# Half of the turned tiles by VectorE in batches 1 to 3, and an order planned with other durations and random shakes

## The chip, the core and the metric

The program runs on one core of a Trainium2 chip. The metric is the device time of one execution in microseconds (us). The core has five engines that work side by side, each through its own list of instructions in order: TensorE (PE) multiplies matrices, VectorE (DVE) and ScalarE (ACT) work on tiles elementwise and along rows, GpSimd (POOL) does elementwise work too, and SyncE (SP) issues the DMA transfers here. An instruction starts when those ahead of it on its engine have been issued and the semaphores it waits for are up.

## The reference

Attention over 4 batches, 8 heads, 576 positions and 64 columns, with a threshold in the softmax, and two feed-forward blocks behind it, all in float32:

```
scores = scale * q @ k.T                     # each batch and head: 576 x 576
thresh = max(scores, -1) - tau
scores = where(scores >= thresh, scores, -1e9)
attn   = softmax(scores);  x = attn @ v      # x: 2304 tokens x 512
h = x @ w_in;  x = (h * clip(h + 3, 0, 6) / 6) @ w_out      # 512 -> 2048 -> 512
h = x @ w_in2; x = (h * sigmoid(1.702 * h)) @ w_out2
```

## The kernel before

**Tiles and stages.** Two heads are one unit, a head pair; there are 4 batches of 4 head pairs. A head pair has nine score tiles of 128 queries by 576 keys: four of its first panel (queries 0 to 255 of both heads), four of its second panel (256 to 511), and a rest tile with the last 64 queries of both. For each tile PE makes the scores (`ps`), DVE takes the row maximum (`nm`, L621) and a threshold from it (`th`), ACT the exponential (`e`, L626), DVE masks it and sums (L627), POOL divides (L640). The tile must then be turned, keys onto partitions, into the buffer `et`, and PE multiplies it with v (`av`, L737, in batch 0; `av_`, L756, in the other batches). The feed-forward blocks work on the transposed result: the first half of block 1 (`moe_a`) runs beside the attention of the next batch, its second half (`moe_b`) and block 2 (`moe2`) behind attention. There each product of two float32 numbers is three matmuls of their high and low parts.

**Turning.** PE turns 128 x 128 pieces with the identity as the other operand (`trans`, L678) into a PSUM bank, and ACT copies the bank to `et` (L681). The other way is `blocks`: DVE turns 32 x 32 blocks of four tiles into the tile `tr` (L699), SP writes `tr` to a scratch tensor in DRAM (`turned`, L702) and reads it back in four transfers, so that the blocks come to lie in their place in `et` (L704); only the last 64 keys go over PE (`last_keys`). `TURNED = (2, 3)` names the batches in which both panels of every head pair go this second way; batch 1 takes `plain`, where PE turns all, and batch 0 has a function of its own, `turn`. In the batches of `TURNED` the threshold is made by ACT (L623), else by DVE (L625). From batch 1 on there is one `et` buffer, `ets[1]`, for all head pairs, five buffers for `e` and three for the raw q and k tiles (`qk`, loaded at L545 and L546).

**What sets the order.** Nothing is executed where it is written. `add` and `move` enter each operation into a plan with its engine, a cost in ns, a nominal time and the buffers that it reads and writes; a `move` enters SP's issue (590 ns) and a transfer whose cost is its bytes divided by 360. `Plan.order` plays the plan through, each engine taking the ready operation with the lowest key; `Plan.latest` plays it backwards and gives new keys. `settle` does both three times, and then, for each seed in `KICKS`, shakes the keys within a random stretch of the plan with `kicked` and does both again. `KICKS` is empty here. `fill` puts dummy products of the tile `two` (L1135) into every gap of PE in the plan that is wide enough. The order so found is fixed when the program is built.

Of the kernel before, what the change touches and what calls it, by code (L numbers as in the profile page):

```python
# [32 lines left out]

KICKS = ()

# [226 lines left out]
def tile_top_attention_moe_moe2(  # L262
# [87 lines left out]
    def pe(n):  # L350
        return 7 + 0.43 * n

# [132 lines left out]
    QC = S + 64  # L485
    TURNED = (2, 3)
    turns = [(dram.tile([P, 2048], F32, name="turned"), mark()) for _ in range(2)]
# [8 lines left out]

    def et_m(p):
        return ets[1].t[:, 2560 * p:2560 * p + 2048].rearrange("p (a h k t j) -> p a h k t j", a=4, h=2, k=4, t=2)

    def et_p(p):  # L500
        return ets[1].t[:, 2560 * p:2560 * p + 2048].rearrange("p (h k n) -> p h k n", h=2, k=4)

    def et_4(p):
        return ets[1].t[:, 2560 * p + 2048:2560 * p + 2560].rearrange("p (h n) -> p h n", h=2)

    def et_r():
        return ets[1].t[:, 5120:].rearrange("p (h k n) -> p h k n", h=2, k=5)

# [3 lines left out]
    def unit(u, b, j, t0):  # L512
# [4 lines left out]
        def K(name, s=0):  # L517
            return t0 + 2700 * s + NOMINAL[name]
# [63 lines left out]
        def score1(s):  # L582

            ps, (hd, m) = buf("ps", 2, "ps", [P, 2, 512]), tiles[s]
            q0 = 256 * hd + m * P

            def mm():
                for i in range(2):
                    nc.tensor.matmul(ps.t[:, i, :SH], f32(qzb.t)[:, q0:q0 + P], f32(khb.t)[:, i * SH:(i + 1) * SH], start=True, stop=True)

            add(PE, 4 * 243, K("S", s), "S", mm, [(qzb, x) for x in (("z", hd), (hd, 0))] + [khb], [ps])
            soft(s, ps)

        def score(ss):

            if len(ss) == 1 and tiles[ss[0]] is not None:
                return score1(ss[0])
            pss = {s: buf("ps", 2, "ps", [P, 2, 512]) for s in ss}

            def mm():  # L600
                for i in range(2):
                    for s in ss:
                        t = tiles[s]
# [3 lines left out]
            add(PE, 4 * 243 + 300 + 40 * (len(ss) > 1), K("S", ss[0]), "S", mm, [qhb, khb], [pss[s] for s in ss])  # L607
            for s in ss:
                soft(s, pss[s])

        def soft(s, ps):
# [9 lines left out]
            add(DVE, 665, K("R", s), "R", lambda: nc.vector.tensor_reduce(out=nm.t[:, c], in_=ps.t[:, :, :SH], op=ALU.max, axis=AX.XY, negate=True), [ps], [(nm, s)])  # L621
            if b in TURNED:
                add(ACT, 150, K("TH", s), "TH", lambda: nc.scalar.activation(out=th.t[:, c], in_=nm.t[:, c], func=ACTF.Identity, scale=-1.0, bias=nt_b.t), [(nm, s), nt_b], [(th, s)])  # L623
            else:
                add(DVE, 121, K("TH", s), "TH", lambda: nc.vector.tensor_scalar(out=th.t[:, c], in0=nm.t[:, c], scalar1=-1.0, scalar2=nt_b.t, op0=ALU.mult, op1=ALU.add), [(nm, s), nt_b], [(th, s)])  # L625
            add(ACT, 624, K("X", s), "X", lambda: nc.scalar.activation(out=ev(), in_=ps.t[:, :, :SH], func=ACTF.Exp, bias=nm.t[:, c]), [ps, (nm, s)], [e])  # L626
# [55 lines left out]

        def last_keys(p, ss):
            trans([(s, 4, tiles[s][0] * 256 + tiles[s][1] % 2 * P) for s in ss], 512, lambda kn: (et_4(p)[:kn], lambda x: x.rearrange("p (h n) -> p h n", h=2)), ets[1], (p, 4), ss[-1])

        def plain(p, ss):
            for hd in range(2):
                mine = [s for s in ss if tiles[s][0] == hd]
                for k0 in (0, 2):
                    trans([(s, k0 + i, i * 256 + m * P) for i in range(2) for m, s in enumerate(mine)], 512,  # L690
                          lambda kn, hd=hd, k0=k0: (et_p(p)[:kn, hd, k0:k0 + 2], lambda x: x.rearrange("p (k n) -> p k n", k=2)), ets[1], (p, hd, k0), ss[-1])
            last_keys(p, ss)

        def blocks(p, ss):

            et, at, src = ets[1], ss[-1], buf("tr", 1, "tr", [P, 4, 2, 4, 2, 32])
            for s in ss:
                hd, t = tiles[s]
                add(DVE, dve(512), K("DT", s), "DT", lambda hd=hd, t=t % 2, e=e_of[s]: nc.vector.transpose(out=src.t[:, :, hd, :, t, :].rearrange("p g k j -> p k g j"), in_=e.t[:, :512].rearrange("p (k g j) -> p k g j", k=4, g=4)),  # L699
                    [e_of[s]], [(src, s)])  # L700
            turned, there = turns[p]
            move(K("DM", at), "DM", 16 * P * 512, lambda: nc.sync.dma_start(out=turned, in_=src.t.rearrange("p g h k t j -> p (g h k t j)")), [src], [there])  # L702
            for g in range(4):
                move(K("DM", at) + 3000, "DM", 4 * P * 512, lambda g=g: nc.sync.dma_start(out=ets[1].t[32 * g:32 * g + 32, 2560 * p:2560 * p + 2048].rearrange("p (a n) -> p a n", a=4),  # L704
                     in_=turned[:, 512 * g:512 * g + 512].rearrange("(a p) n -> p a n", a=4)), [there], [(et, ("m", p, g))])
            last_keys(p, ss)

        def turn_r():

            et, at = ets[1], 4  # L710
            trans([(4, k, k * P) for k in range(4)], 512,
                  lambda kn: (et_r()[:kn, :, 0:4].rearrange("p h k n -> p k h n"), lambda x: x.rearrange("p (k h n) -> p k h n", k=4, h=2)), et, "r", at)
            trans([(4, 4, 0)], P, lambda kn: (et_r()[:kn, :, 4], lambda x: x.rearrange("p (h n) -> p h n", h=2)), et, "r4", at)

        def turn(p, ss, rest):

            et, at = ets[0], ss[-1]
            for hd in range(2):
# [10 lines left out]
        def av(p, at):  # L729
# [8 lines left out]

            op = add(PE, 350 + 10 * (1 + 0.84 * n), K("AV", at), "AV", mm, [vs] + [(et, r) for r in regions], [pv], [xr])
            add(ACT, act(n), K("XR", at), "XR", copy(lambda: xr.t, lambda: pv.t[:, :n]), [pv], [xr])  # L740
            return op

        def av_(at):

            et, pv = ets[1], [bank(1), bank(1)]
            for x in pv:
                add(PE, 0, K("AV", at), "AV", lambda: None, [vs, et], [x], xrs.values())

            def mm():
                def x(p, k, hd):  # L750
                    return et_r()[:, hd, k] if p == 2 else et_4(p)[:, hd] if k == 4 else et_p(p)[:, hd, k] if b not in TURNED else et_m(p)[:, :, hd, k].rearrange("p a t j -> p t a j")

                for p, o, c, n in ((0, pv[0], 0, 256), (1, pv[0], 256, 256), (2, pv[1], 0, 64)):
                    for k in range(5):
                        for hd in range(2):
                            nc.tensor.matmul(o.t[64 * hd:64 * hd + 64, c:c + n], v_(k, hd), x(p, k, hd), start=k == 0, stop=k == 4)  # L756

            add(PE, 450 + 10 * (2 + 0.84 * S), K("AV", at), "AV", mm, [vs, et], pv, xrs.values())
            add(ACT, act(256), K("XR", at), "XR", copy(lambda: xrs[0].t, lambda: pv[0].t[:, :256]), [pv[0]], [xrs[0]])
            add(ACT, act(256), K("XR", at), "XR", copy(lambda: xrs[1].t[:, :256], lambda: pv[0].t[:, 256:]), [pv[0]], [(xrs[1], 0)])  # L760
            add(ACT, act(64), K("XR", at), "XR", copy(lambda: xrs[1].t[:, 256:], lambda: pv[1].t[:, :64]), [pv[1]], [(xrs[1], 1)])

# [10 lines left out]
        def full():  # L773
            for p in range(2):
                if p:
                    score2(4)
                for pair in PAIRS[p]:
                    for s in pair:
                        score2(s)
                    norm(([4] if pair[0] == 5 else []) + list(pair))  # L780
                    if pair[0] == 5:
                        turn_r()
# [281 lines left out]
    for b in range(B):  # L1064
# [9 lines left out]
        if u == FULL:  # L1074
# [6 lines left out]
            changed[-1][0].deps |= {o for o in pl.ops if any(x.pool == "stg" for x in o.bufs)}  # L1081
            for ap, r in ((lambda: et_4(0)[64:], (0, 4)), (lambda: et_4(1)[64:], (1, 4)), (lambda: et_r()[64:, :, 4], "r4")):
                add(POOL, 124 + 1.04 * 512, t, "ez", lambda ap=ap: nc.gpsimd.memset(ap(), 0.0), [], [(ets[1], r)])
        else:
# [109 lines left out]
```

## Time and profile before

| | |
|---|---|
| median of 3 runs | 1097.37 us (1097.24 to 1100.8) |
| the profiled execution | 1093.03 us, its span 1091.2 us |
| PE busy | 1058.7 us, 97% of the span |
| DVE / ACT / POOL busy | 724.2 / 638.1 / 515.3 us |
| attention ends | at about 440.7 us |

A profile is one execution. Its rows give busy times of engines, idle times with what ended them (`<-`), the chain of work that ended last, and for a DMA the time from its issue to its landing. Matmuls overlap in the array, so the duration of one (0.27 us for 128 columns) is longer than the distance from one to the next, and busy time counts overlapping ones once. A float32 product that isn't marked fp32r in the program has two records for one instruction; transposes have one. The clock column is the granted TensorE clock as a share of full speed.

### The profile page before, as it was taken

The page shows a single profiled execution, that of the slowest core. Times are in us where ns is not written, and L with a number is a line of the kernel's source. Part 1 is how long each engine was busy: PE and PEld are TensorE (multiplying, and loading weights), DVE is VectorE, ACT ScalarE, POOL GpSimd, SP SyncE. Part 2 cuts the span into 40 slices and gives each one's busy share as a digit, 9 for nine tenths or more (in the row PEclk, how much of TensorE's full clock was granted, in tenths as well). Part 3 has the DMA queues.
Part 4 walks back from the last instruction along what each step waited for, and adds up shares of the span by engine and source line. Part 5 has one row for each costly group of instructions (what it writes and reads, how often), then busy time and mean ns, then how long its engine had stood idle before and what let it go on. Part 6 is the DMA issues. An engine that isn't in the chain of part 4 may idle for free.

```text
span 1091.2 us, 20840 instructions
## 1 busy us (share of the span) xinstructions
PE 1058.7 (97%) x7706; PEld 970.0 (89%) x7706; DVE 724.2 (66%) x1485; ACT 638.1 (58%) x1340; POOL 515.3 (47%) x598
## 2 busy tenths in 40 slices
PE   8999899989898999999999999999999999999998
PEld 7677788888787989999999999989998989889888
DVE  6998766676686784467877333778787675563634
ACT  4888777765576664576555324666566665444433
POOL 3679868675686764555466224541323332001000
PEclk9999999999999999999999999999999999999999
DMA  7334222266878687445654212435545543312202
GB/s 206 116 120 129 96 68 78 91 190 176 250 213 271 200 242 195 140 137 166 203 174 145 79 48 61 132 105 183 175 137 173 167 139 102 116 46 71 92 1 73
DMA packets 90053, 150.19 MB, mean 138 GB/s; under 512 B 8928, under 2 KB 51552, under 8 KB 87904
## 3 DMA queue, kind: packets, MB, share of 16 engines
q1 hardware_dynamic: 89952, 148.87, 44.8%
q8 instruction: 60, 0.98, 0.4%
q14 instruction: 41, 0.34, 0.1%
HBM read 101.52 MB, written 47.32 MB: 136 GB/s over the span
## 4 chain that ended last, share of the span: by engine, by line
PE 69%; DVE 9%; DMA 7%; ACT 5%; POOL 4%; issue 3%; SPq 2%; POOLq 0%; DVEq 0%; ACTq 0%
PE py L835 23%; PE pm L815 14%; PE pm L972 14%; PE pm L835 6%; PE pm L756 4%; PE ps L573 4%; PE pm L678 2%; DMA qk<-in_k_dram 2%; DVE e L627 2%; DMA qk<-in_q_dram 1%; ACT e L626 1%; DVE nm L621 1%; DMA wrawstg<-in_w1i_dram 1%; POOL e L640 1%; POOL kqv L369 1%
## 5 line engine op out<-in xcount | busy, mean ns | idle before, releaser
L835 PE MATMUL py<-g,outhring 128*128 128x512 f32 (+2 forms) x1152 | 287.7, 337 | 2.6 <-DVE g L369 1.3
L835 PEld LDWEIGHTS py<-g,outhring 128*128 128x128 f32 x1152 | 193.7, 188 | 20.6 <-DVE g L369 3.3
L835 PE MATMUL py<-g,outlring 128*128 128x512 f32 (+2 forms) x576 | 193.5, 336 | 0.0
L815 PE MATMUL pm<-xh,inhring 128*128 128x256 f32 (+1 forms) x512 | 154.8, 302 | 2.3 <-DVE t L827 2.2
L815 PE MATMUL pm<-xl,inhring 128*128 128x256 f32 (+1 forms) x512 | 151.8, 296 | 0.0
L815 PE MATMUL pm<-xh,inlring 128*128 128x256 f32 (+1 forms) x512 | 151.7, 296 | 0.0
L972 PE MATMUL pm<-outhring,inhring 128*128 128x256 f32 x512 | 144.5, 282 | 1.5 <-ACT u L366 0.8
L972 PE MATMUL pm<-outlring,inhring 128*128 128x256 f32 x512 | 143.6, 281 | 0.0
L972 PE MATMUL pm<-outhring,inlring 128*128 128x256 f32 x512 | 143.5, 280 | 0.0
L621 DVE TENSOR_REDUCE nm<-ps 128x1 f32<-128x576 f32 x144 | 106.2, 750 | 34.4 <-PE ps L573 30.3
L369 POOL TENSOR_TENSOR g<-t,g 128x256 fp32r<-128x256 f32 (+1 forms) x104 | 88.1, 851 | 82.7 <-ACT g L366 79.9
L627 DVE SCALAR_TENSOR_TENSOR e<-ps,th,e 128x576 f32<-128x576 f32 x128 | 102.6, 810 | 33.2 <-ACT e L626 31.9
L827 DVE SCALAR_TENSOR_TENSOR t<-t,pm 128x256 f32<-128x256 f32 (+1 forms) x128 | 57.1, 448 | 94.0 <-ACT t L826 93.7
L835 PEld LDWEIGHTS py<-g,outlring 128*128 128x128 f32 x576 | 108.2, 188 | 10.0
L369 POOL TENSOR_TENSOR wmstg<-wmstg,wrstg 128x512 uint32<-128x512 uint32 x48 | 64.6, 1347 | 94.8 <-DVE wmstg L422 77.3
L835 PE MATMUL pm<-g,outhring 128*128 128x256 f32 (+1 forms) x512 | 107.7, 301 | 0.5 <-POOL g L369 0.4
L369 POOL TENSOR_TENSOR g<-tc,g 128x512 fp32r<-128x512 f32 x24 | 31.8, 1326 | 161.6 <-ACT g L366 154.9
L826 ACT ACTIVATE t<-pm,half 128x256 f32<-128x256 f32 (+1 forms) x128 | 63.7, 498 | 74.3 <-PE pm L815 68.6
L626 ACT ACTIVATE e<-ps,nm 128x576 f32<-128x576 f32 x128 | 93.0, 733 | 15.2 <-DVE nm L621 13.4
L815 PEld LDWEIGHTS pm<-xh,inhring 128*128 128x128 f32 x512 | 98.0, 191 | 4.2 <-DVE t L827 2.9
L972 PEld LDWEIGHTS pm<-outhring,inhring 128*128 128x128 f32 x512 | 96.8, 189 | 4.9 <-ACT u L366 1.1
L972 PEld LDWEIGHTS pm<-outlring,inhring 128*128 128x128 f32 x512 | 96.9, 189 | 2.6
(114 smaller groups left out, 2433.8 us busy)
## 6 DMA issues: line engine op xcount, KB each, us to landing
turned<-tr SPq DMA_DIRECT2D x16, 1024.0 KB, 4.5
et<-turned SPq DMA_DIRECT2D x64, 256.0 KB, 5.6
wrawstg<-in_w1i_dram SPq DMA_DIRECT2D x16, 512.0 KB, 4.0
wrawstg<-in_w1o_dram SPq DMA_DIRECT2D x16, 512.0 KB, 3.8
wrawstg<-in_w2i_dram SPq DMA_DIRECT2D x16, 512.0 KB, 3.9
wrawstg<-in_w2o_dram SPq DMA_DIRECT2D x16, 512.0 KB, 3.9
qk<-in_k_dram SPq DMA_DIRECT2D x24, 288.0 KB, 3.9
qk<-in_q_dram SPq DMA_DIRECT2D x24, 288.0 KB, 3.7
```

What stands on the lines that cost most here:

```text
L369: return lambda: (nc.vector if eng == DVE else nc.gpsimd).tensor_tensor(out=o(), in0=a(), in1=b(), op=op)
L573: nc.tensor.matmul(ps.t[:, i, :SH], qss[hd].t[:, q0:q0 + P], w[hd].t[:, i * SH:(i + 1) * SH], start=a, stop=z)
L621: add(DVE, 665, K("R", s), "R", lambda: nc.vector.tensor_reduce(out=nm.t[:, c], in_=ps.t[:, :, :SH], op=ALU.max, axis=AX.XY, negate=True), ...
L626: add(ACT, 624, K("X", s), "X", lambda: nc.scalar.activation(out=ev(), in_=ps.t[:, :, :SH], func=ACTF.Exp, bias=nm.t[:, c]), [ps, (nm, s)] ...
L627: add(DVE, 729, K("M", s), "M", lambda: nc.vector.scalar_tensor_tensor(out=ev(), in0=ps.t[:, :, :SH], scalar=th.t[:, c], in1=ev(), op0=ALU ...
L678: nc.tensor.transpose(pt.t[:kn, o:o + P], e_of[s].t[:, keys(k)], id_b.t)
L756: nc.tensor.matmul(o.t[64 * hd:64 * hd + 64, c:c + n], v_(k, hd), x(p, k, hd), start=k == 0, stop=k == 4)
L815: nc.tensor.matmul(ph.t[:, :n], a, v, start=(cc == 0 and i == 0), stop=(cc == KC - 1 and i == 2))
L826: add(ACT, 93 + act(n), K("RL"), "RL", lambda: nc.scalar.activation(out=tt_(), in_=pt(), func=ACTF.Relu, scale=1.0 / 6.0, bias=half_b.t), ...
L827: add(DVE, dve(n), K("GT"), "GT", lambda: nc.vector.scalar_tensor_tensor(out=tt_(), in0=tt_(), scalar=1.0, in1=pt(), op0=ALU.min, op1=ALU. ...
L835: nc.tensor.matmul(py.t[:, :n], a, v, start=(st and i == 0), stop=(sp and i == 2))
L972: nc.tensor.matmul(o.t[:, :n], u.t[:, ws], v.t[:, xv], start=(st and kk == 0 and i == 0), stop=(sp and kk == 1 and i == 2), skip_group_che ...
```

## The change

Three things change together. In batches 1 to 3 the first panel of each head pair goes by `blocks` (DVE and DRAM), and the second panel and the rest tile by `turn` (PE and ACT), where batch 1 had both panels on PE and batches 2 and 3 both on DVE. With it, `av_` multiplies two groups of 256 and 320 queries instead of three of 256, 256 and 64, and all thresholds are made by DVE. Second, costs of the plan are other numbers. Third, `KICKS` holds nine seeds.

```
-KICKS = ()
+KICKS = (9, 22, 44, 100, 235, 395, 771, 940, 4389)
...
 def pe(n):
-        return 7 + 0.43 * n
+        return 9 + 0.428 * n
...
-    TURNED = (2, 3)
...
-            if b in TURNED:
-                add(ACT, 150, K("TH", s), "TH", lambda: nc.scalar.activation(out=th.t[:, c], in_=nm.t[:, c], func=ACTF.Identity, scale=-1.0, bias=nt_b.t), [(nm, s), nt_b], [(th, s)])
-            else:
-                add(DVE, 121, K("TH", s), "TH", lambda: nc.vector.tensor_scalar(...
+            add(DVE, 121, K("TH", s), "TH", lambda: nc.vector.tensor_scalar(...
...
             for g in range(4):
-                move(K("DM", at) + 3000, "DM", 4 * P * 512, ...
+                move(K("DM", at) + 3000, "DM", 7 * P * 512, ...
...
-            op = add(PE, 350 + 10 * (1 + 0.84 * n), K("AV", at), "AV", mm, ...
+            op = add(PE, 150 + 10 * (1 + 0.84 * n), K("AV", at), "AV", mm, ...
...
-                for p, o, c, n in ((0, pv[0], 0, 256), (1, pv[0], 256, 256), (2, pv[1], 0, 64)):
+                for p in range(2):
                     for k in range(5):
                         for hd in range(2):
-                            nc.tensor.matmul(o.t[64 * hd:64 * hd + 64, c:c + n], v_(k, hd), x(p, k, hd), start=k == 0, stop=k == 4)
+                            x = et_a(et, 1, hd, k) if p else et_4()[:, hd] if k == 4 else et_0()[:, :, hd, k].rearrange("p a t j -> p t a j")
+                            nc.tensor.matmul(pv[p].t[64 * hd:64 * hd + 64, :CH[p][1]], v_(k, hd), x, start=k == 0, stop=k == 4)
...
-                (blocks if b in TURNED else plain)(p, ss)
+                if p:
+                    turn(p, ss, 4)
+                else:
+                    blocks(ss)
```

SP's queue in batch 2, before: `turned<-tr` is the write of a panel that DVE has turned, `et<-turned` one of the four reads of it, `qk` and `kqv` the loads of q, k and v of head pairs to come.

```order
L702 DMA turned<-tr 128x2048
L704 DMA et<-turned 32x4x512 x4
L545 DMA qk<-in_k_dram 128x576
L702 DMA turned<-tr 128x2048
L853 DMA ypd<-ys 128x256 x2
L702 DMA turned<-tr 128x2048
L704 DMA et<-turned 32x4x512 x4
L546 DMA qk<-in_q_dram 128x576
L704 DMA et<-turned 32x4x512 x4
L545 DMA qk<-in_k_dram 128x576
```

The same queue in batch 2 of the changed kernel, where line numbers are smaller by 7 to 30:

```order
L681 DMA turned<-tr 128x2048
L539 DMA qk<-in_q_dram 128x576
L736 DMA x1d<-xr_3283 128x256
L823 DMA ypd<-ys 128x256
L683 DMA et<-turned 32x4x512 x4
L552 DMA kqv<-in_vp_dram 128x640
L538 DMA qk<-in_k_dram 128x576
L823 DMA ypd<-ys 128x256
L539 DMA qk<-in_q_dram 128x576
L538 DMA qk<-in_k_dram 128x576
L823 DMA ypd<-ys 128x256
L681 DMA turned<-tr 128x2048
```

One round trip per head pair stands there where two stood, and whole groups of q and k loads lie between two round trips.

PE at the end of batch 3, before: the last product with v (`pm<-et,kqv`), the last products of `moe_a` around it (`pm<-g,out...`), and the dummies (`pm<-two`) ahead of the next stage.

```order
L835 MATMUL pm<-g,outhring_1416 128x320 x2
L835 MATMUL pm<-g,outlring_1440 128x320
L756 MATMUL pm<-et,kqv 64x256 x20
L756 MATMUL pm<-et,kqv 64x64 x10
L835 MATMUL pm<-g,outhring_1530 128x320 x2
L835 MATMUL pm<-g,outlring_1541 128x320
L835 MATMUL pm<-g,outhring_1598 128x320 x2
L835 MATMUL pm<-g,outlring_1611 128x320
L1135 MATMUL pm<-two 128x128 x4
```

The same end in the changed kernel, from the transposes of the last second panel (`pm<-id,e`):

```order
L668 MATMUL pm<-id,e 128x128 x16
L805 MATMUL pm<-g,outhring_1145 128x320 x2
L805 MATMUL pm<-g,outlring_1168 128x320
L668 MATMUL pm<-id,e 64x128 x4
L805 MATMUL pm<-g,outhring_1231 128x320 x2
L805 MATMUL pm<-g,outlring_1244 128x320
L805 MATMUL pm<-g,outhring_1328 128x320 x2
L805 MATMUL pm<-g,outlring_1342 128x320
L726 MATMUL pm<-et,kqv 64x256 x10
L726 MATMUL pm<-et,kqv 64x320 x10
```

Sixteen transposes that DVE did before now stand on PE in each head pair of batches 2 and 3, and the product with v has two shapes of ten instructions instead of thirty instructions; two dummies (`L1105 MATMUL pm<-two`) stand in this place instead of four.

## Rows read from the trace of the kernel before

**Rows 1.** The page: busy time of TensorE and its weight loads, share, instructions.

```profile
PE 1058.7 (97%) x7706; PEld 970.0 (89%) x7706; DVE 724.2 (66%) x1485; ACT 638.1 (58%) x1340; POOL 515.3 (47%) x598
```

**Rows 2.** Stretches: length, busy PE, PEld, DVE, ACT, POOL, clock, DMA share, GB/s.

```profile
0.00:123.60 123.60, 114.42 (x780) 88.61 (x780) 105.69 (x255) 93.71 (x176) 85.20 (x117) 1.00 0.43 132
123.60:224.00 100.40, 97.82 (x818) 88.02 (x818) 65.55 (x166) 71.09 (x147) 73.48 (x103) 1.00 0.27 84
224.00:338.70 114.70, 105.36 (x844) 95.26 (x840) 84.30 (x179) 70.59 (x168) 79.86 (x111) 0.97 0.80 228
338.70:440.70 102.00, 97.84 (x811) 89.80 (x807) 67.62 (x144) 60.43 (x144) 61.62 (x87) 0.98 0.74 212
440.70:620.00 179.30, 178.10 (x1359) 177.50 (x1359) 120.42 (x234) 99.95 (x206) 100.96 (x88) 1.00 0.50 152
```

**Rows 3.** Stretches of the dummy products (L1135) alone: length, busy PE (records).

```profile
0.00:123.60 123.60, 12.07 (x74) 1.00 0.43 132
...
440.70:1091.20 650.50, 6.12 (x42) 1.00 0.38 119
```

**Rows 4.** TensorE's timeline: start, duration, instruction, [idle time before it, releaser].

```profile
238.88 0.94 PE L678 MATMUL pm<-id,e 128*64 128x128 f32 x4 [2.03 <-ACT et L681]
...
277.06 1.30 PE L573 MATMUL ps<-kqv 128*128 128x288 f32 x4 [3.41 <-DVE e L627]
...
301.05 0.41 PE L815 MATMUL pm<-xh,inhring 128*128 128x320 f32 x1 [1.71 <-DVE t L827]
...
354.15 0.79 PE L573 MATMUL ps<-kqv 128*128 128x288 f32 x4 [2.99 <-DVE e L627]
```

**Rows 5.** Stretches of 20 us around these waits, columns as in rows 2.

```profile
240.00:260.00 20.00, 19.34 (x147) 18.09 (x147) 17.03 (x40) 13.38 (x32) 14.61 (x23) 0.94 0.53 157
260.00:280.00 20.00, 16.59 (x138) 15.42 (x135) 9.41 (x19) 8.74 (x21) 8.73 (x12) 0.91 0.93 226
300.00:320.00 20.00, 18.73 (x149) 15.94 (x150) 17.89 (x39) 15.22 (x37) 16.91 (x23) 1.00 0.64 180
340.00:360.00 20.00, 16.21 (x117) 15.75 (x116) 14.47 (x31) 13.69 (x34) 14.98 (x21) 0.91 0.81 234
```

**Rows 6.** The chain that ended last, batches 2 and 3: start, duration, what.

```profile
230.85 7.11 DMA qk<-in_k_dram
...
265.12 8.56 DMA qk<-in_q_dram
...
343.46 7.68 DMA qk<-in_k_dram
```

**Rows 7.** DMA issues, KB each, us to landing: 124 to 224 us, then 224 to 440.

```profile
qk<-in_q_dram SPq DMA_DIRECT2D x8, 288.0 KB, 2.9
...
qk<-in_q_dram SPq DMA_DIRECT2D x12, 288.0 KB, 6.4
qk<-in_k_dram SPq DMA_DIRECT2D x11, 288.0 KB, 6.0
```

**Rows 8.** The chain again: products with v, and four transposes.

```profile
54.07 2.31 PE pm L737 x20
...
120.76 2.84 PE pm L737 x20
...
313.43 5.05 PE pm L756 x60
...
322.58 0.44 PE pm L678 x4
```

**Rows 9.** Stretch of batch 1, PE's transposes (L678) alone: length, busy PE (records).

```profile
123.60:224.00 100.40, 24.68 (x180) 1.00 0.27 84
```

**Rows 10.** Groups by line on ACT and DVE: busy, mean ns, idle before.

```profile
L681 ACT ACTIVATE et<-pm 128x512 f32<-128x512 f32 (+2 forms) x128 | 66.5, 551 | 17.0 <-PE pm L678 14.8 <-PE pm L756 1.8
L623 ACT ACTIVATE th<-nm,nt 128x1 f32<-128x1 f32 x72 | 20.9, 290 | 25.2 <-DVE nm L621 24.7
L699 DVE STREAM_TRANSPOSE tr<-e 128x512 f32<-128x512 f32 x64 | 44.0, 700 | 5.1 <-POOL e L640 4.9
L625 DVE TENSOR_SCALAR th<-nm,nt 128x1 f32<-128x1 f32 x72 | 14.1, 209 | 0.6
```

More of the change, by code (lines that the diff above doesn't have):

```diff
@@ L495, in et_all, with et_0, et_4 @@
         return et.t[:, (0, 2560)[p]:(2560, 5760)[p]].rearrange("p (h k n) -> p h k n", h=2, k=5)
[L497 to L507, printed above, removed]
+    def et_0():
+        return ets[1].t[:, :2048].rearrange("p (a h k t j) -> p a h k t j", a=4, h=2, k=4, t=2)
+    def et_4():
+        return ets[1].t[:, 2048:2560].rearrange("p (h n) -> p h n", h=2)
     for p in range(2):
@@ L589, in mm @@
                     nc.tensor.matmul(ps.t[:, i, :SH], f32(qzb.t)[:, q0:q0 + P], f32(khb.t)[:, i * SH:(i + 1) * SH], start=True, stop=True)
-            add(PE, 4 * 243, K("S", s), "S", mm, [(qzb, x) for x in (("z", hd), (hd, 0))] + [khb], [ps])
+            add(PE, 4 * 243 + 60, K("S", s), "S", mm, [(qzb, x) for x in (("z", hd), (hd, 0))] + [khb], [ps])
             soft(s, ps)
@@ L605, in mm @@
                         nc.tensor.matmul(pss[s].t[:, i, :SH], f32(qhb.t)[rows, q0:q0 + P], f32(khb.t)[rows, i * SH:(i + 1) * SH], start=True, stop=True)
-            add(PE, 4 * 243 + 300 + 40 * (len(ss) > 1), K("S", ss[0]), "S", mm, [qhb, khb], [pss[s] for s in ss])
+            add(PE, 4 * 243 + 200, K("S", ss[0]), "S", mm, [qhb, khb], [pss[s] for s in ss])
             for s in ss:
@@ L621, in soft @@
             add(DVE, 665, K("R", s), "R", lambda: nc.vector.tensor_reduce(out=nm.t[:, c], in_=ps.t[:, :, :SH], op=ALU.max, axis=AX.XY, negate=True), [ps], [(nm, s)])
-            if b in TURNED:
-                add(ACT, 150, K("TH", s), "TH", lambda: nc.scalar.activation(out=th.t[:, c], in_=nm.t[:, c], func=ACTF.Identity, scale=-1.0, bias=nt_b.t), [(nm, s), nt_b], [(th, s)])
-            else:
-                add(DVE, 121, K("TH", s), "TH", lambda: nc.vector.tensor_scalar(out=th.t[:, c], in0=nm.t[:, c], scalar1=-1.0, scalar2=nt_b.t, op0=ALU.mult, op1=ALU.add), [(nm, s), nt_b], [(th, s)])
+            add(DVE, 121, K("TH", s), "TH", lambda: nc.vector.tensor_scalar(out=th.t[:, c], in0=nm.t[:, c], scalar1=-1.0, scalar2=nt_b.t, op0=ALU.mult, op1=ALU.add), [(nm, s), nt_b], [(th, s)])
             add(ACT, 624, K("X", s), "X", lambda: nc.scalar.activation(out=ev(), in_=ps.t[:, :, :SH], func=ACTF.Exp, bias=nm.t[:, c]), [ps, (nm, s)], [e])
@@ L681, in trans, with blocks @@
             add(ACT, act(size), K("EH", at), "EH", lambda: nc.scalar.activation(out=dst(kn)[0], in_=dst(kn)[1](pt.t[:kn, :size]), func=ACTF.Copy), [pt], [(et, tag)])
[L683 to L694, printed above, removed]
+        def blocks(ss):
             et, at, src = ets[1], ss[-1], buf("tr", 1, "tr", [P, 4, 2, 4, 2, 32])
@@ L698, in blocks @@
                 hd, t = tiles[s]
-                add(DVE, dve(512), K("DT", s), "DT", lambda hd=hd, t=t % 2, e=e_of[s]: nc.vector.transpose(out=src.t[:, :, hd, :, t, :].rearrange("p g k j -> p k g j"), in_=e.t[:, :512].rearrange("p (k g j) -> p k g j", k=4, g=4)),
+                add(DVE, dve(512), K("DT", s), "DT", lambda hd=hd, t=t, e=e_of[s]: nc.vector.transpose(out=src.t[:, :, hd, :, t, :].rearrange("p g k j -> p k g j"), in_=e.t[:, :512].rearrange("p (k g j) -> p k g j", k=4, g=4)),
                     [e_of[s]], [(src, s)])
-            turned, there = turns[p]
+            turned, there = turns[u % 2]
             move(K("DM", at), "DM", 16 * P * 512, lambda: nc.sync.dma_start(out=turned, in_=src.t.rearrange("p g h k t j -> p (g h k t j)")), [src], [there])
             for g in range(4):
[L704 to L713, printed above, removed]
+                move(K("DM", at) + 3000, "DM", 7 * P * 512, lambda g=g: nc.sync.dma_start(out=ets[1].t[32 * g:32 * g + 32, :2048].rearrange("p (a n) -> p a n", a=4),
+                     in_=turned[:, 512 * g:512 * g + 512].rearrange("(a p) n -> p a n", a=4)), [there], [(et, ("m", g))])
+            trans([(s, 4, tiles[s][0] * 256 + tiles[s][1] * P) for s in ss], 512, lambda kn: (et_4()[:kn], lambda x: x.rearrange("p (h n) -> p h n", h=2)), et, (0, 4), at)
         def turn(p, ss, rest):
-            et, at = ets[0], ss[-1]
+            et, at = ets[not early], ss[-1]
             for hd in range(2):
@@ L737, in mm @@
                         nc.tensor.matmul(pv.t[64 * hd:64 * hd + 64, :n], v_(k, hd), et_a(et, p, hd, k), start=k == 0, stop=k == 4)
-            op = add(PE, 350 + 10 * (1 + 0.84 * n), K("AV", at), "AV", mm, [vs] + [(et, r) for r in regions], [pv], [xr])
+            op = add(PE, 150 + 10 * (1 + 0.84 * n), K("AV", at), "AV", mm, [vs] + [(et, r) for r in regions], [pv], [xr])
             add(ACT, act(n), K("XR", at), "XR", copy(lambda: xr.t, lambda: pv.t[:, :n]), [pv], [xr])
@@ L749, in mm @@
             def mm():
-                def x(p, k, hd):
-                    return et_r()[:, hd, k] if p == 2 else et_4(p)[:, hd] if k == 4 else et_p(p)[:, hd, k] if b not in TURNED else et_m(p)[:, :, hd, k].rearrange("p a t j -> p t a j")
-                for p, o, c, n in ((0, pv[0], 0, 256), (1, pv[0], 256, 256), (2, pv[1], 0, 64)):
+                for p in range(2):
                     for k in range(5):
                         for hd in range(2):
-                            nc.tensor.matmul(o.t[64 * hd:64 * hd + 64, c:c + n], v_(k, hd), x(p, k, hd), start=k == 0, stop=k == 4)
[L758 to L761, printed above, removed]
+                            x = et_a(et, 1, hd, k) if p else et_4()[:, hd] if k == 4 else et_0()[:, :, hd, k].rearrange("p a t j -> p t a j")
+                            nc.tensor.matmul(pv[p].t[64 * hd:64 * hd + 64, :CH[p][1]], v_(k, hd), x, start=k == 0, stop=k == 4)
+            add(PE, 200 + 10 * (2 + 0.84 * S), K("AV", at), "AV", mm, [vs, et], pv, xrs.values())
+            for p in range(2):
+                add(ACT, act(CH[p][1]), K("XR", at), "XR", copy(lambda p=p: xrs[p].t, lambda p=p: pv[p].t[:, :CH[p][1]]), [pv[p]], [xrs[p]])
         def xsplit(s, p):
@@ L780, in full @@
                     norm(([4] if pair[0] == 5 else []) + list(pair))
-                    if pair[0] == 5:
-                        turn_r()
                 ss = [s for pair in PAIRS[p] for s in pair]
-                (blocks if b in TURNED else plain)(p, ss)
+                if p:
+                    turn(p, ss, 4)
+                else:
+                    blocks(ss)
             av_(ss[-1])
@@ L1081, in tile_top_attention_moe_moe2 @@
             changed[-1][0].deps |= {o for o in pl.ops if any(x.pool == "stg" for x in o.bufs)}
-            for ap, r in ((lambda: et_4(0)[64:], (0, 4)), (lambda: et_4(1)[64:], (1, 4)), (lambda: et_r()[64:, :, 4], "r4")):
-                add(POOL, 124 + 1.04 * 512, t, "ez", lambda ap=ap: nc.gpsimd.memset(ap(), 0.0), [], [(ets[1], r)])
+            add(POOL, 124 + 1.04 * 512, t, "ez", lambda: nc.gpsimd.memset(et_4()[64:], 0.0), [], [(ets[1], (0, 4))])
+            add(POOL, 124 + 2.08 * 320, t, "ez", lambda: nc.gpsimd.memset(et_all(ets[1], 1)[64:, :, 4, :], 0.0), [], [(ets[1], x) for x in ((1, 4), "r4")])
         else:
```

## The prediction, made before the changed kernel was run

> **What bounds the kernel now.** I read the share of busy time first, then the stretches by batch of attention, then, inside the poor stretches, TensorE's timeline with its idle times, the granted clock, the chain that ended last, and the DMA issues.
>
> TensorE (PE) is busy for 97% of the span [rows 1], so an edit pays only if it takes work from PE or fills its gaps. The stretches [rows 2] end where the last product with v of a batch ends. Between 440.7 and 620 us, behind attention, PE is busy for 178.1 of 179.3 us: nothing to win. In batches 0, 1, 2 and 3 it lacks 9.2, 2.6, 9.3 and 4.2 us. Part of "busy" is not work either: the kernel puts dummy products of the tile `two` (L1135) where its plan sees a gap, and these take 12.07 us in batch 0 and 6.12 us behind attention [rows 3].
>
> In batches 2 and 3 the gaps are few and long. Four waits, of 2.03, 3.41, 1.71 and 2.99 us [rows 4], make 10.1 us. Three are followed by a lower granted clock: the 20 us slices that hold or follow them show 0.94, 0.91 and 0.91, while the slice with the 1.71 us wait shows 1.00 [rows 5]. Below full clock (2.4 GHz, the low level being 1.2) PE has lost about 20 x (0.06 + 0.09 + 0.09) = 4.8 us there. Together 14.9 us.
>
> The chain leads from these waits to loads: a k load of 7.11 us ends just before the 2.03 us wait, a q load of 8.56 us before the 3.41 us one, and a k load of 7.68 us before the 2.99 us one [rows 6]. The same q loads land in 2.9 us in batch 1 but in 6.4 us in batches 2 and 3, k loads in 6.0 us [rows 7]. What differs is the DMA share: 0.27 in batch 1, where PE turns everything, against 0.80 and 0.74 where VectorE (DVE) turns the tiles and sends them through DRAM [rows 2]. So DRAM round trips in batches 2 and 3 delay the next pair's loads, and these starve PE.
>
> **The change part by part.** Today there are 16 round trips (two for each of eight head pairs); the changed kernel has 12, one for each head pair of batches 1 to 3.
>
> 1. PE transposes. 128x128 transposes of `e` go from 256 to 320: 64 fewer in batch 1, 128 more in batches 2 and 3. Four cost 0.44 us on the chain [rows 8], so 0.11 us each, and 64 x 0.11 = **+7.0 us**. From below, the pure issue: 180 of them kept PE busy for 24.68 us in batch 1 with overlapping tails [rows 9], at most 0.137 each, which makes the upper end 8.8; the lower end, if all 64 fell into idle time that is there anyway, is 0. All lie on PE, so I take 7.0.
>
> 2. Product with v. It is cut into 256 + 320 columns instead of 256 + 256 + 64: the same columns. Today one takes 5.05 us for 60 records; the two shapes of the new one stand in batch 0 at 2.31 and 2.84 us [rows 8], 5.15 together. Twelve times 0.1 is **+1.2 us**; the lower end is 0.
>
> 3. DVE and ScalarE (ACT). DVE gives up 32 block transposes in batches 2 and 3, 32 x 0.70 = 22.4 us, and takes over 72 thresholds from ACT, 72 x 0.209 = 15.0 us; batch 1 gets 16 x 0.70 = 11.2 us, so DVE stands there at 65.55 + 11.2 = 76.8 of 100.4 us, no more crowded than in batch 2 (84.3 of 114.7). ACT gives up 72 x 0.29 = 20.9 us and gets 32 evictions of turned tiles more in batches 2 and 3, 32 x 0.551 = 17.6 us [rows 2, 10]. I cost all of it at 0: the cover is the quarter of each batch in which these engines idle. Without cover PE would wait for a bank as in the 2.03 us wait, behind ACT's `et` [rows 4].
>
> 4. DMA waits. Above batch 1's level the round trips cost (0.80 - 0.27) x 114.7 + (0.74 - 0.27) x 102 = 109 us of all DMA engines, 6.8 us each. Four per batch over some 105 us add 0.26, so the share becomes about 0.53 in all three batches, near the 0.50 of the stretch behind attention, where PE hardly waits. SP's queue also loses four reads per head pair ahead of the next q and k. If landing goes halfway, (2.9 + 6.2) / 2 = 4.5 us, loads come 1.7 us earlier: the waits of 1.71 and 2.03 shrink to about 0.3, 3.41 and 2.99 to 1.7 and 1.3; 3.3 stay and 6.8 go. The clock's 4.8 us go too, since a 1.71 us wait had no drop behind it. What is late next is in batch 1, whose loads now come later; I set against it one wait of the 1.71 size with its surroundings, 2.0. Sum 6.8 + 4.8 - 2.0: **-9.6 us**; ends 0 and -14.9.
> The Trainium skill (DMA: Bandwidth & Descriptors, "Latency and other measured facts") puts memory access at 0.2 us on average and 2 us at high load. Estimated from that page alone, a load could lose at most 1.8 us to load and win back 0.9, so the four waits would give 3.6 instead of 6.8. The rows show a rise of 3.1 to 3.5 us, so the measurement decides.
>
> 5. Fillers. In the order, dummy products fall from 65 to 49: 37 to 30 in batch 0, 5 to 7 in batch 1, 2 and 2, and 21 to 10 behind attention. The trace counts two records for each, 0.163 us in batch 0 and 0.146 behind attention [rows 3]. So 7 x 2 x 0.163 + 11 x 2 x 0.146 less 2 x 2 x 0.15 is **-4.9 us**, if the plan's gaps are gone on the chip as well; 0 if PE then simply stands idle.
>
> 6. The rest of the order. New durations and nine shakes shift instructions everywhere, and no row prices that. At best it wins the 9.2 us of idle time in batch 0; at worst it brings one more wait of 3.41 us with 1.8 us of lost clock (a slice at 0.91), 5.2. No row is nearer to either end, so I take the middle, **-2.0 us**.
>
> Sum: 7.0 + 1.2 - 9.6 - 4.9 - 2.0 = -8.3. The profiled execution, 1093.03 us with a span of 1091.2, would become 1084.7. It lies 4.3 us below the median of the runs, 1097.37, so I forecast 1097.4 - 8.3, **1089 us**.
>
> **The rivals.** A, slower: the loads stay late because of their place in SP's queue, not because of mean load. For it: the 8.56 us load was issued right behind four reads of a turned tile, and in the new order k or q still follows the four reads of ten of the twelve round trips. Then all three batches pay what batches 2 and 3 pay now, 14.9 / 2 = 7.5 each, 7.5 more in all; the gaps and their dummies stay; 7.0 + 1.2 + 7.5 = +15.7, 1113 us. Against it: batch 3, with almost the same share, loses less than batch 2. It decides once q and k land later than about 5 us in all three batches.
> The Trainium skill (same page, "Queues, rings and completion order") says that SP owns one row of rings on the 16 engines, each consumed in ring order. By that rule it is the transfers ahead that count, as in A; the 8.56 us row agrees, the 2.9 us of batch 1, where nothing large stands ahead, does not contradict it.
>
> B, no change: PE stops waiting for loads but meets the softmax chain or ACT's evictions, since a pair of batches 2 and 3 now needs eight evictions where it needed four. Half of part 4's gain (5.8, less the 2.0 in batch 1) and half of the fillers (2.5): 8.2 - 3.8 - 2.5 = +1.9, 1099 us. For it: DVE, ACT and GpSimd are at 59 to 74% in those batches, so a wait is never far [rows 2].
>
> C, a larger gain: all 14.9 us go without a new wait in batch 1, and the order takes 5.6 us, midway between my 2.0 and its end of 9.2: 8.2 - 14.9 - 4.9 - 5.6 = -17.2, 1080 us. For it: a turned tile now travels while the pair's second panel is still in softmax, and the second panel needs no DMA at all before the product with v.
>
> That the change would not do what it says is excluded by the order: twelve writes of turned tiles, four for each batch.
>
> **How the numbers follow.** The forecast gets 0.38 (its own range 1084 to 1095), C 0.22, B 0.25, A 0.15. The range goes from 1074, where C meets the far end of part 6, to 1108, which leaves out half of A. A measurement of this kernel can tell about 0.5%, 5.5 us: faster is below 1091.9, slower above 1102.9. Faster: C and most of the forecast, 0.56; same: most of B and the forecast's edge, 0.27; slower: A and B's tail, 0.17.
>
> **What would show it.** In the changed profile: q and k landing at about 4.5 us in batches 1 to 3 and a DMA share near 0.53 (part 4); no PE wait over 2 us and a granted clock of 1.00 in those batches; L1135 some 5 us shorter with no new idle time in its place (part 5); transposes 7 us longer. I am wrong if loads still land at 6 us (A), if waits for ACT's `et` or DVE's `e` grow to some 10 us (B), or if batch 1 grows by as much as batch 2 shrinks.

## The result, and the profile after

The changed kernel takes 1081.88 us (median of 4 runs, 1081.44 to 1084.38) against 1098.61 us of the kernel before on the same chip; the ratio is 0.9855, with a 95% interval of 0.9831 to 0.9879. Measured once more, it was 0.9829 (0.9788 to 0.9871). So it is faster by 1.5 to 1.7%, some 16 to 19 us, where 8.3 were forecast.

The profiled execution has a span of 1082.5 us. The stretches by batch, cut as in [rows 2] at the last product with v of a batch, and the columns as there; the last row is all that lies behind attention:

```profile
0.00:124.40 124.40, 112.81 (x757) 87.26 (x757) 105.48 (x257) 94.14 (x176) 84.48 (x117) 0.99 0.45 131
124.40:216.40 92.00, 90.61 (x680) 79.16 (x679) 72.80 (x180) 62.21 (x121) 73.57 (x102) 1.00 0.64 184
216.40:323.40 107.00, 106.33 (x819) 95.33 (x817) 75.74 (x187) 69.40 (x139) 76.90 (x106) 1.00 0.55 156
323.40:427.20 103.80, 103.74 (x804) 93.44 (x804) 70.40 (x178) 65.74 (x129) 65.11 (x92) 1.00 0.46 137
427.20:1082.50 655.30, 644.09 (x4445) 606.75 (x4445) 408.90 (x742) 342.82 (x707) 216.11 (x182) 1.00 0.38 119
```

PE lacks 1.4, 0.7 and 0.1 us in batches 1, 2 and 3, where it lacked 2.6, 9.3 and 4.2, and the clock is 1.00 in all three. The waits of [rows 4] are gone: this is all that PE waited for in batches 2 and 3 (engine, tile, line, what it waited for: us in total, times, longest).

```profile
PE ps L566 <- DVE e L617: 0.5, 1, 0.5
PE pm L668 <- POOL e L630: 0.2, 1, 0.2
```

The loads of q and k in batches 2 and 3 land in 4.2 and 3.2 us instead of 6.4 and 6.0 [rows 7]:

```profile
qk<-in_q_dram SPq DMA_DIRECT2D x12, 288.0 KB, 4.2
qk<-in_k_dram SPq DMA_DIRECT2D x11, 288.0 KB, 3.2
```

The dummy products fell as the order said, in batch 0 and behind attention (busy PE, records), against 12.07 and 6.12 us in [rows 3]:

```profile
0.00:124.40 124.40, 10.63 (x60) 0.99 0.45 131
...
427.20:1082.50 655.30, 3.18 (x20) 1.00 0.38 119
```

Nothing came of it in this profile: batch 0 took 124.4 us instead of 123.6 [rows 2], and what lies behind attention 655.3 us instead of 650.5.

**A measure that allows for moved work.** Batches can't be compared by length alone, since the order moves feed-forward products from one to another. So I take PE's work out: the instructions that stand in a stretch by the order, times the distance from one start to the next where PE ran undisturbed in the trace of before (0.119, 0.1465 and 0.2275 us for a feed-forward product of 256, 320 and 512 columns, 0.1315 for a score product, 0.0885 for a transpose, 0.2245 for 256 columns of v). The figure for a transpose is the mean of a group of four, whose successor starts 0.03 us behind the last of them; two transposes in a row start 0.109 us apart. What is left of the stretch is PE's loss there: waiting, dummies, a lower clock, late weights. It is an estimate, good to some 2 us for a stretch. The total work is 1002.6 us before and 1008.2 us after.

| PE's loss, us | batch 0 | batch 1 | batches 2 and 3 | behind | span |
|---|---|---|---|---|---|
| before, first profile | 35.7 | 11.4 | 27.1 | 14.4 | 1091.2 |
| before, second profile | 36.6 | 12.4 | 29.2 | 14.9 | 1095.7 |
| changed, first profile | 37.6 | 8.7 | 9.2 | 18.7 | 1082.5 |
| changed, second profile | 33.7 | 8.8 | 8.7 | 15.0 | 1074.5 |

The gain lies in batches 2 and 3: about 19 us, of which the 5.6 us of added work take back a third. The two profiles of the changed kernel differ by 8 us, and only in batch 0 and behind attention. In those two columns a difference of less than 4 us carries no weight, and each kernel of the experiments below has one profile only.

### The profile page after: what moved, and what is told of

Its sections match the earlier page's. It is cut to its first block, busy times and chain, and to the rows that moved or that the text cites. A ratio compares the mean times of both kernels' runs of the same rounds, so it can differ in the third digit from the quotient of the medians.

```text
span 1082.5 us, 20424 instructions
## 1 busy us (share of the span) xinstructions
PE 1057.6 (98%) x7498; PEld 961.9 (89%) x7498; DVE 733.3 (68%) x1541; ACT 634.3 (59%) x1272; POOL 516.2 (48%) x597
## 4 chain that ended last, share of the span: by engine, by line
PE 77%; DMA 8%; DVE 5%; POOL 3%; ACT 2%; SPq 2%; issue 2%; DVEq 0%; POOLq 0%; ACTq 0%
PE py L805 25%; PE pm L942 15%; PE pm L785 15%; PE pm L805 7%; PE pm L726 6%; PE ps L566 5%; PE pm L668 3%; DMA qk<-in_q_dram 1%; DMA kept<-wmstg 1%; DMA et<-turned 1%; DMA wrawstg<-in_w1i_dram 1%; POOL wmstg L369 1%; DMA yc<-ypd 1%; DMA wrawstg<-in_w1o_dram 1%; DVE nm L614 1%
## 5 line engine op out<-in xcount | busy, mean ns | idle before, releaser
L369 POOL TENSOR_TENSOR g<-tc,g 128x512 fp32r<-128x512 f32 x24 | 32.4, 1351 | 157.5 <-ACT g L366 135.8
```

The source lines that it names most:

```text
L369: return lambda: (nc.vector if eng == DVE else nc.gpsimd).tensor_tensor(out=o(), in0=a(), in1=b(), op=op)
```

## The experiments

In each, lines not shown are as in the kernel named, and `...` stands for what is left out of a line. Ratios are to the kernel before on the same chip.

### Both kernels once more

No edit. The first profiles of the two kernels differ by 8.7 us and their medians by 16.7.

> The kernel before, unchanged, for a second profile of it: the two profiles shown differ by 8.7 us in span while the medians differ by 16.7. If the first profile was a short execution of the same program, this one shows a span nearer 1096 us, with the missing 5 us in longer waits of batches 2 and 3 (loads). If it is again 1091 us, the missing time lies outside the span.

1096.36 us, ratio 0.9992 (0.9973 to 1.0011), span 1095.7. The 4.5 us more are spread: 0.9 in batch 0, 1.0 in batch 1, 2.1 in batches 2 and 3, 0.5 behind. The first profile had been a short execution, and the span accounts for the time.

> The changed kernel once more, for a second profile: its first profile showed 655.3 us behind attention where the same order showed 651.3 with transposes done twice. If that is chance of an execution, this one shows 651 to 653 and a span near 1078; if the order does it, 655 again.

1079.91 us, span 1074.5. Two of its stretches, batch 0 and behind attention:

```profile
0.00:120.50 120.50, 109.83 (x757) 84.74 (x757) 104.69 (x257) 93.59 (x176) 84.51 (x117) 1.00 0.45 135
...
422.90:1074.50 651.60, 642.61 (x4445) 606.07 (x4445) 409.76 (x742) 342.54 (x707) 217.76 (x182) 1.00 0.38 119
```

Same order, 651.6 instead of 655.3 us: the slow end of the first profile was chance of an execution. A pair of profiles told half the gain here; the medians, and stretches seen in two profiles, told the rest.

### The three parts of the change, apart

The changed kernel without shakes:

```
-KICKS = (9, 22, 44, 100, 235, 395, 771, 940, 4389)
+KICKS = ()
```

> The changed kernel with KICKS empty: half of the tiles turned on DVE and the new durations stay, only the shakes go. Theory 1 (the gain is the DRAM round trips that no longer starve PE, spread over three batches): most of the 16.7 us stays, 1084 to 1089 us, q and k still land in 3 to 4.5 us. Theory 2 (the searched order is the gain): 1094 us or more, with more dummy products and new waits of PE.

1091.03 us, ratio 0.9957 (0.9939 to 0.9975): between the two theories.

That kernel with the old durations as well, so that only the split of the turning is left:

```
-        return 9 + 0.428 * n
+        return 7 + 0.43 * n
...
-                move(K("DM", at) + 3000, "DM", 7 * P * 512, ...
+                move(K("DM", at) + 3000, "DM", 4 * P * 512, ...
```

(and the old costs of scores and products with v)

> The changed kernel with KICKS empty and the old durations in the plan: only the split of the turning stays. Theory 1: 1085 to 1091 us, 8 to 13 us under the kernel before. Theory 2: no gain or a loss, 1097 to 1106 us, because 64 more transposes cost 7 us and nothing orders them better.

1102.39 us, ratio 1.0048 (1.0031 to 1.0064): slower than before. Theory 1 is wrong on this point.

The kernel before with the new durations (the same lines the other way):

> The kernel before with the new durations in its plan and nothing else: both panels on DVE in batches 2 and 3, KICKS empty. Theory 1: within 4 us of before (1094 to 1102), since the loads stay at 6 us. Theory 2 in its other form (a truer plan is the gain, above all the dearer reads of turned tiles): 1088 to 1092 us and shorter waits for q and k.

1099.49 us, ratio 1.0021 (0.9998 to 1.0045): nothing.

The kernel before, shaken with seeds searched for its own plan:

```
-KICKS = ()
+KICKS = (1, 11, 338, 1139, 1226, 1269, 1414, 4302)
```

> The kernel before with eight seeds in KICKS, searched for its own plan and its old durations; the turning stays as it was. Theory 1 (the split frees PE of waits in batches 2 and 3, and the shakes then close the hole that the split leaves in batch 1): shakes on the old split give little, at most 4 us, 1092 to 1097, and the waits for q and k in batches 2 and 3 stay. Theory 2 (the search is worth its 9 us on any split): 1085 to 1089.

1084.25 us, ratio 0.9902 (0.9883 to 0.9920): 11.7 us from the shakes alone, on the old split. Theory 2 holds here, with a little more than it said. And "half only", shaken with fourteen seeds searched for that plan:

```
-KICKS = ()
+KICKS = (1, 25, 95, 97, 172, 804, 1233, 1471, 1501, 1626, 1677, 1729, 2715, 2997)
```

> Half of the tiles turned on DVE as in the changed kernel, the old durations in the plan, and fourteen seeds searched for that plan. So far the shakes gave 11.7 us on the old split and 11 on the new one with new durations, and the new durations gave 11.4 on the new split without shakes. Theory 1 (durations and shakes mend the same hole in batch 1): 1080 to 1085 us, as good as the changed kernel within 0.4%. Theory 2 (they add up): 1089 to 1093.

1090.23 us, ratio 0.9929 (0.9907 to 0.9952): theory 2. On the new split durations and shakes add up: the durations give 0.9% without shakes (1.0048 to 0.9957) and 0.9% with them (0.9929 to 0.984). Last, the changed kernel with other seeds:

```
-KICKS = (9, 22, 44, 100, 235, 395, 771, 940, 4389)
+KICKS = (10007, 10016, 10028, 10075)
```

> The changed kernel with four other seeds, found from a later start, that leave the plan about as short as the nine do. Theory 1 (a shorter plan carries over to the chip): 1079 to 1085 us. Theory 2 (the nine seeds happen to suit the chip, whatever the plan says): 1086 to 1092, like no shakes at all.

1084.13 us, ratio 0.9875 (0.9825 to 0.9925): theory 1. The nine seeds are not a lucky find; another search of the same plan gives about as much.

| ratio to before | no shakes | shaken |
|---|---|---|
| both panels on DVE, old durations | 1 | 0.9902 |
| both panels on DVE, new durations | 1.0021 | not run |
| half, old durations | 1.0048 | 0.9929 |
| half, new durations | 0.9957 | 0.9855, 0.9829; other seeds 0.9875 |

Shakes give 1.0 to 1.3% in each row where both were run, 0.8% with the other seeds. The split alone loses 0.3 to 0.5% (0.3 between the two shaken kernels, whose intervals overlap); with the new durations it gains 0.4 to 0.7%. The losses of PE tell where:

| PE's loss, us | batch 0 | batch 1 | batches 2 and 3 | behind |
|---|---|---|---|---|
| half only | 39.4 | 24.4 | 12.1 | 16.1 |
| half and new durations | 35.7 | 17.2 | 12.2 | 18.9 |
| all three (changed, two profiles) | 37.6, 33.7 | 8.7, 8.8 | 9.2, 8.7 | 18.7, 15.0 |
| before, shaken | 35.5 | 12.4 | 18.3 | 14.2 |
| before, durations only | 38.1 | 15.6 | 22.1 | 21.4 |
| half, old durations, shaken | 32.4 | 14.2 | 16.8 | 17.2 |

The split by itself takes 15 to 17 us of loss out of batches 2 and 3 and puts 12 to 13 into batch 1. There the loads of k landed in 2.8 us before the change (DMA issues, 124 to 224 us):

```profile
qk<-in_k_dram SPq DMA_DIRECT2D x8, 288.0 KB, 2.8
```

Now they land late in "half only" (chain, start, duration):

```profile
161.80 7.04 DMA qk<-in_k_dram
...
193.99 7.47 DMA qk<-in_k_dram
```

and PE waits behind them (timeline, idle time in brackets):

```profile
170.08 0.30 PE L668 MATMUL pm<-id,er 128*64 128x128 f32 x1 [1.74 <-ACT et L671]
...
202.70 0.66 PE L668 MATMUL pm<-id,e 128*128 128x128 f32 x4 [1.86 <-ACT et L671]
```

Behind the first of these waits the clock is down to 0.66 for ten us:

```profile
170.00:180.00 10.00, 9.23 (x47) 7.97 (x49) 3.47 (x9) 5.85 (x13) 6.11 (x11) 0.66 0.06 23
```

That is one half of it. PE waits for 6.5 us in batch 1 of "half only" where it waited for 2.5, and the clock takes some 3.4 us. The other half is dummies, 29 in batch 1 instead of 5, which `fill` puts where the plan itself has gaps. They take 8.02 us in "half only" (first line; 1.44 us in the kernel before) and 7.44 us with the new durations and no shakes (second line), where no wait in batch 1 is longer than 0.8 us and the clock is 1.00:

```profile
125.70:233.40 107.70, 8.02 (x58) 0.97 0.54 153
...
121.80:222.60 100.80, 7.44 (x58) 1.00 0.58 169
```

In the changed kernel they take 1.89 us. So in batch 1 the new durations took away the waits that the plan had not foreseen, and the shakes the gaps that it had.

Three kernels with the same split, so with the same bytes in batch 1, differ in when k lands there: 6.1 us in "half only", 4.2 us with the new durations, 3.7 us in the changed kernel. These are the k rows of the DMA issues of batch 1 in that order of kernels, first "half only":

```profile
qk<-in_k_dram SPq DMA_DIRECT2D x8, 288.0 KB, 6.1
```

then with the new durations:

```profile
qk<-in_k_dram SPq DMA_DIRECT2D x8, 288.0 KB, 4.2
```

and the changed kernel:

```profile
qk<-in_k_dram SPq DMA_DIRECT2D x8, 288.0 KB, 3.7
```

The DMA share of batch 1 runs the other way, 0.54, 0.58 and 0.64 in the same order, so the landing does not follow the mean load. It fits the place of a load among the round trips, which the plan sets; no run moved one load alone, so that is argued. The shaken kernel before shows the other side: its loads in batches 2 and 3 land as late as ever,

```profile
qk<-in_q_dram SPq DMA_DIRECT2D x12, 288.0 KB, 6.4
qk<-in_k_dram SPq DMA_DIRECT2D x11, 288.0 KB, 5.8
```

and yet the loss there fell by 9 to 11 us. An order can pay for a late load by having other work ready.

### The transfers, with the order held

Half of each round trip in the kernel before:

```
-            move(K("DM", at), ... nc.sync.dma_start(out=turned, in_=src...)...
+            move(K("DM", at), ... nc.sync.dma_start(out=turned[:, :1024], in_=src...[:, :1024])...
...
-                move(K("DM", at) + 3000, ... lambda g=g: nc.sync.dma_start(out=ets[1]..., in_=turned...)...
+                move(K("DM", at) + 3000, ... lambda g=g: g < 2 and nc.sync.dma_start(out=ets[1]..., in_=turned...)...
```

> The kernel before, every engine's order unchanged, but of each turned panel only half the columns are written to DRAM and only two of the four reads are issued, so half of the keys of batches 2 and 3 hold old values. Theory 1 (DMA load starves PE): q and k land in 3 to 4.5 us instead of 6, PE's loss in batches 2 and 3 falls from some 28 us to 13 to 18, 1083 to 1090 us. Theory 3 (the waits come from DVE's 64 block transposes or from the order of the chain, not from the transfers): within 3 us of before.

1081.22 us, ratio 0.9861 (0.9839 to 0.9884), a little below what theory 1 said. The kernel leaves out half of each turned panel, so its result is not the reference's. q and k land in 4.4 and 4.5 us, and the loss in batches 2 and 3 is 12.9 us instead of 27 to 29, with every engine's order as it was:

```profile
225.80:330.40 104.60, 102.25 (x841) 92.54 (x842) 83.94 (x179) 70.29 (x168) 80.05 (x112) 1.00 0.58 165
330.40:428.30 97.90, 96.07 (x807) 88.20 (x807) 67.38 (x144) 59.84 (x144) 61.35 (x86) 1.00 0.49 140
```

DVE is as busy as before (83.9 and 67.4 us against 84.3 and 67.6 in [rows 2]), so theory 3 falls: it is the transfers that starve PE, not DVE's transposes. Two of the four read issues on SP go with the bytes, so this run does not tell bytes from issues.

Each transfer of a round trip once more in the changed kernel:

```
                 nc.sync.dma_start(out=turned, in_=flat)
+                nc.sync.dma_start(out=spare[0], in_=flat)
...
                 nc.sync.dma_start(out=ets[1]..., in_=turned...)
+                nc.sync.dma_start(out=spare[1]..., in_=turned...)
```

> The changed kernel, every engine's order unchanged, with each write and each read of a turned panel issued once more towards scratch in DRAM: 4 MB per head pair, as batches 2 and 3 of the kernel before had. Theory 1: q and k land near 6 us again, PE waits return in all three batches, 15 to 25 us on top of the changed kernel, 1095 to 1107. Theory 3: up to 4 us on top, 1080 to 1085.

1130.83 us, ratio 1.0321 (1.0303 to 1.0340), so some 52 us above the changed kernel (at the mean of its two ratios, 0.9842): in the direction of theory 1, but more than twice its size. q lands in 5.9 us in batches 1 to 3, k at the median in 3.6, no later than in the changed kernel. The copies add one write and four reads to each round trip and as many issues on SP. The chain tells bytes from issues: between 124 and 476 us it holds 66.7 us of loads of q and k, single ones 7 to 8.5 us long, and 10.7 us of SP's issues, where the changed kernel's chain has 12.1 and 4.3 us (124 to 430 us). So here it is mostly late loads. The next run has fewer bytes and more issues.

Straight from `tr` to `et`, in the changed kernel:

```
-            move(K("DM", at), ... nc.sync.dma_start(out=turned, in_=...)...
...
+                for a in range(4):
+                    nc.sync.dma_start(out=ets[1].t[32 * g:32 * g + 32, 512 * a:512 * a + 512], in_=flat[32 * a:32 * a + 32, 512 * g:512 * g + 512])
```

> The changed kernel without the way through DRAM: each of the four reads of a turned panel becomes four transfers of 32 rows straight from tr to et, in the old place of the reads; the write falls away. PE, DVE, ACT and GpSimd keep their order. Half the bytes, but sixteen issues where five stood. Theory 1 (bytes delay the loads): loads land earlier, 2 to 6 us less than the changed kernel, 1074 to 1078. Theory 3 (issues on SP's queue delay them): 0 to 8 us more, 1080 to 1088.

1118.26 us, ratio 1.0179 (1.0138 to 1.0220), some 38 us above the changed kernel, although half the bytes are gone and q and k land in 3.1 and 3.2 us once issued. SP's timeline shows why: sixteen issues hold the queue for 10 us, and the loads of v, k and q come behind them.

```profile
210.14 10.25 SPq L685 DMA_DIRECT2D et<-tr  x16
220.48 0.53 SPq L552 DMA_DIRECT2D kqv<-in_vp_dram  x1
...
222.33 0.38 SPq L538 DMA_DIRECT2D qk<-in_k_dram  x1
```

In the changed kernel the four reads take 1.74 us there:

```profile
198.01 1.74 SPq L683 DMA_DIRECT2D et<-turned  x4
```

The chain agrees: between 124 and 460 us the issues of L685 make up 39.1 us of it, where the reads of the changed kernel (L683) made up 4.2. Both theories named something real, fast landing and issues, and neither named the size: theory 3's issues decide, at 38 us where it allowed 8. A load can land fast and still be late, because it was issued late. The write to `turned` also freed `tr` early, and here DVE waits for the transfers once, for 3.6 us; that share was not taken apart.

### Transposes

In the changed kernel, each group of sixteen full transposes of a second panel twice:

```
-                for s, k, o in parts:
+                for s, k, o in parts * (2 if <full group of a second panel, batches 1 to 3> else 1):
```

> The changed kernel with each group of sixteen full transposes of a second panel done twice into the same bank: 192 transposes more on PE, order otherwise unchanged. At the 0.11 us of the prediction: 21 us on top of the changed kernel, 1102; at the pure issue interval of 0.09, 17 us; if they fall into idle time, under 8.

1096.92 us, ratio 1.0017 (1.0003 to 1.0031). By its two ratios the changed kernel would stand at 1077.2 or 1080.0 us there, so 192 transposes cost 17 to 20 us, 0.09 to 0.10 us each; the intervals of the ratios allow 3 to 5 us either way. In the trace PE's transposes in batches 1 to 3 take 70.0 us instead of 49.6, 0.106 us for each one added. All of it lies on the path: the loss of PE fell by no more than the measure's error (batches 1 to 3: 19.2 us at 0.0885 us for a transpose, 15.3 at 0.109 for the added ones, against 17.9 and 17.5).

## Why the prediction was right or wrong

The direction, the range and the place of the gain were right; the size was half, and two terms were wrong. The range's lower end, 1074, does not follow from its own terms: C with part 6 at its far end is 7.0 + 1.2 - 14.9 - 4.9 - 9.2 = -20.8, so 1076.6.

**Part 1 (transposes, +7.0).** Right. At 0.09 to 0.11 us each, 64 cost 5.7 to 7.0 us.

**Part 2 (product with v, +1.2).** Nothing: one now takes 5.07 us in the timeline, 5.12 before.

**Part 3 (DVE and ACT at 0).** Right for the changed kernel: its waits for ACT's `et` in batches 1 to 3 are 0.5 us or less, though DVE is more crowded in batch 1 than I said (my own 76.8 of 100.4 us is 76%, against 73% in batch 2; it became 72.8 of 92.0, 79%). Without shakes and new durations it is not: there PE waited for `et` in batch 1, behind late loads.

**Part 4 (waits for loads, -9.6).** That round trips delay the loads and these starve PE was right and was shown with the order held: half the transfers took 14 to 16 us of loss out of batches 2 and 3. The split alone took 15 to 17, near my upper end of 14.9. Two steps failed. The landing does not follow the DMA share: I had 0.53 and 4.5 us for all three batches; the shares are 0.64, 0.55 and 0.46, q and k land in 3.3 and 3.7 us in batch 1, 4.2 and 3.2 in batches 2 and 3, and batch 1 of the three kernels above runs against it. And the price of batch 1, "one wait of the 1.71 size, 2.0", was too low: by itself the split costs batch 1 some 12.5 us, about half of it waits and clock behind late loads, half dummies in gaps of the plan. The new durations bring that down to 5.3, and the shakes on top turn it into a gain of 3. Split and durations without shakes change the loss by -16.0 in batches 2 and 3 and +5.3 in batch 1, together -10.7; that my -9.6 comes near is luck, since gain and price were both too small.

**Part 5 (fillers, -4.9).** Wrong. The dummies fell by 4.4 us [rows 3], but batch 0 and the stretch behind attention lose as much as before (36 and 15 us, against 34 to 38 and 15 to 19). PE stands idle instead: 11.6 us in batch 0 and 11.2 behind (10.7 and 9.0 in the second profile), against 9.2 and 7.3 before. The lower end, 0, was right.

**Part 6 (the order, -2.0).** This is the term that was most mis-sized. I priced it by the idle time of batch 0 alone and took the middle. The shakes give 11 to 12 us on the old split and on the changed one, and none of it in batch 0: without them the changed kernel loses 8.5 us more in batch 1, 5.5 of it in dummies, and 3 more in batches 2 and 3. On "half only" 7 of the 11 us do lie in batch 0. On the old split the row that would have told was the same as that of part 4: where a load is late, the order decides what PE has to do meanwhile, so all 27 us of loss in batches 2 and 3 were open to it, not just the idle time of batch 0. That is my reading of the shaken kernel before, whose loads stayed late.

So the sum came out low since two errors of opposite sign, part 5 (4.9 too much gain) and part 6 (9 to 10 too little), don't balance. By stages, mean of two profiles each: batch 0 -0.5, batch 1 -3.2, batches 2 and 3 -19.2, behind +2.2, work +5.6, together -15.

**The rivals.** A said that place in SP's queue counts and not the mean load. It did not come true for the whole change, but its mechanism did in part: late loads are about half of what makes the split alone slower, and the direct transfers show it at its plainest. The Trainium skill (DMA: Bandwidth & Descriptors, "Queues, rings and completion order") has SP's transfers on one row of rings, taken in ring order; the k loads of 6.1, 4.2 and 3.7 us with equal bytes agree with it. My rule that A decides at a landing of 5 us for q and k in all three batches was not tested: in "half only", which is slower, only k in batch 1 lands later (6.1 us; q 4.8). B did not occur. C was nearest in time (1080), and its first part was right (all waits went), its way to the rest not (the dummies gave nothing, and the order 11 to 12 us where C had 5.6), so that its time came so near is luck.

**Not settled.** Which of the new durations matters was not tried; that it is the dearer read (1.27 us in the plan instead of 0.73) fits the earlier landing of k, but is only argued, and with the old durations and shakes k lands in 3.4 us in batch 1 too. The kernel before with new durations and shakes was not run.

No kernel tried beat the changed one: other seeds reached 0.9875, direct transfers lost.

## What to carry to other kernels

Where a fixed order is planned, a transfer's price has two parts, its bytes and the time its issues hold the queue for what comes behind. I would issue a load that something waits for ahead of a bulk round trip, not behind it; no run here tried that by itself. Don't move a bulk transfer into a stretch that had none without replanning that stretch: here the same edit was worth +0.5% alone and -0.4% with a plan of the new durations. A search over orders that keeps what shortens the plan can carry over to the chip (1.0 to 1.3% on three plans), and two profiles of each kernel are needed before stretches are compared.

## What the runs showed that was not expected

A DMA issue of 64 KB from 32 partitions held SP for about 0.64 us (10.25 us for sixteen in a row) where a load of 288 KB over 128 partitions mostly took 0.33 to 0.38 us. One more write and four more reads per round trip, its own transfers once more, cost 4.3 us of the program's time for each of the twelve trips (52 us in all). A wait of 1.74 us, with one of 0.69 us soon behind it, stood ahead of ten us at a clock of 0.66 in "half only", while the wait of 1.71 us in the kernel before had no drop behind it [rows 5]; part 4 had taken that one for the rule. And a program whose engines run in one fixed order still varied by 8 us between two undisturbed executions.
